# PV summed every three steps, VectorE blocks one by one, FFN values copied out of PSUM early, and fewer steps per run, in a two-layer attention and FFN kernel

## The chip, the cores and the metric

The kernel runs on one core of a Trainium2 chip. A core has a matrix engine (PE, with its weight loads listed apart as PEld), VectorE (DVE), ScalarE (ACT), GpSimd (POOL) and a DMA queue (SP), which run side by side (in the profile of the kernel before PE was busy for 89% of the span, DVE for 65%, ACT for 94% and POOL for 68%) and wait for each other by semaphores. The metric is the device time of one launch in microseconds (us), lower is better. A ratio is the mean time of one kernel's fast runs over the mean time of the other's in the same rounds, so it is not quite the ratio of the medians quoted.

## The reference, cut to what matters

Two layers; each is attention over 2048 tokens with 32 heads of width 16, then an FFN of width 1792, both with a residual and a layernorm in front. The weights are the same in both layers.

```python
x = A_x                                   # 1 x 2048 x 512, bf16
x = x + attention(layernorm(x), wqkv, wo) # 32 heads, Dh = 16, softmax over 2048 keys
x = x + silu(layernorm(x) @ w1) @ w2      # 512 -> 1792 -> 512
x = x + attention(layernorm(x), wqkv, wo)
x = x + silu(layernorm(x) @ w1) @ w2
```

With 32 heads, 2048 queries and 2048 keys, one layer has 134 million exponentials. They are the bulk of the work.

## The kernel before

The kernel is one long software pipeline. Queries go in *chunks* of 512; there are four chunks a layer, so eight in all. A chunk is worked off in eight *runs* of four heads each (four lanes, one per head). In a run each lane has 16 blocks of 128 keys x 512 queries, so a full run has 64 blocks. About three quarters of the blocks get their exponential on ACT, two in each *step*. The others ("VectorE blocks") get an approximation of the exponential: VectorE computes a number whose bits, read as fp16, are a rough exponential (the y tile), and POOL makes two shifted versions of it (the z tiles). PE then sums all three against V and two scaled copies of V. So a run of 24 steps has 48 ACT blocks and 16 VectorE blocks; a run of 23 steps has 46 and 18.

Everything else (layernorm, projections, the output projection, the FFN) is background work: Python generators that yield between pieces. A small model of PE, DVE and ACT decides in which step a piece is put; it is part of the kernel's Python and fixes the instruction order before anything runs. The model knows nothing of POOL.

The parts that the change and the argument touch:

```python
STEPS = {16: (24, 23), 12: (20, 20), 8: (12, 12), 4: (7, 7)}   # keys' blocks: steps
...
t1 = t0 + STEPS[len(kts)][not (0, 1) <= key[0:2] <= (1, 0)]     # key[0:2]: layer, chunk
...
ends = [*range(t0 + 2, t1 - 1, 2), t1]       # PV every two steps
for a, b in zip([t0, *ends], ends):
    pv[b + 1] = list(range(a, b))
```

```python
def emit_d(t, blk):                          # one VectorE block in step t
    s_ps = psum["s"].tile([P, 512], FP32, name="d_ps", tag="sd", bufs=2)
    score(blk, s_ps[:])
    if not pairs or len(pairs[-1]["ds"]) == 2:
        y = dpool.tile([P, 2, 512], U16, name="d_y", tag="y", bufs=Y_BUFS)
        pairs.append(dict(ds=[], y=y))
    ...                                      # nc.vector.tensor_scalar -> one half of y
    if len(pr["ds"]) == 2 or blk == last_d:
        other_terms(t, pr)

def other_terms(t, pr):                      # POOL, once for a pair: 128 x 1024
    for k, (off, _) in enumerate(TERMS):     # two terms
        z = dpool.tile([P, 2, 512], U16, name=f"d_z{k}", tag=f"z{k}")
        nc.gpsimd.tensor_scalar(out=z..., in0=pr["y"]..., scalar1=float(off), scalar2=1.0,
                                op0=ALU.add, op1=ALU.mult)
```

```python
# PV: 'real' groups of four matmuls side by side (starts some 3 ns apart in the trace before);
# 'fill' groups multiply by zeros only to keep PE busy, which is meant to hold its clock (with
# more of them PV by three ran at a clock of 0.991 instead of 0.936, below; FULL_CLOCK = 3
# groups for two steps)
fill = math.ceil(FULL_CLOCK - busy - real) if real > 1 else 0
fill = max(0, min(fill, 2))
...
# FFN: h = w1 part; tanh read from PSUM; multiply reads PSUM and SBUF
h_ps = yield from mm4("h_ps", ..., out=0)
t_sb = tpool.tile([P, 512], FP32, name="t_sb", tag="t")      # one buffer
silu_tanh(h_ps, t_sb[:])                                     # ACT
yield part(0.6, held=True)
silu_mul(ft, h_ps, t_sb[:], hT)                              # VectorE: (t + 1) * h
```

The softmax here doesn't subtract the row's maximum and nothing guards it: scores larger than these inputs give would overflow.

## Time and profile before

| kernel before | |
|---|---|
| median of 4 runs | 1616.74 us (1610.56 to 1624.54) |
| span of the profiled run | 1605.9 us |
| ACT busy | 94% |
| PE busy | 89% |
| POOL busy | 68% |
| DVE busy | 65% |
| mean granted TensorE clock of the profiled run | 0.986 |
| exponentials on ACT, VectorE blocks, POOL z operations | 1552, 992, 992 |

The page's table of busy times, and three of its costliest groups. In a group line the columns are: line of the kernel, engine, operation, output and input tiles, shapes, count, then busy us and mean ns of one, then the idle time of the engine just before them and what ended most of it.

```profile
PE 1436.8 (89%) x12965; PEld 439.9 (27%) x12965; DVE 1036.7 (65%) x1729; ACT 1514.0 (94%) x1671; POOL 1098.4 (68%) x1160
...
L1020 ACT ACTIVATE p_sb<-s_ps 128x1024 bf16<-128x1024 f32 x1552 | 1464.9, 1047 | 47.4 <-PE s_ps L754 26.7
...
L836 PE MATMUL o_ps<-w_qkv,zero 128*32 128x512 bf16 x570 | 113.1, 383 | 0.0
...
L526 ACT ACTIVATE t_sb<-h_ps 128x512 f32<-128x512 f32 x98 | 60.3, 615 | 0.0
```

ACT is the engine that sets the time: 1552 exponentials, 47.4 us of waiting before them in the whole run. The 570 matmuls against a tile named zero are the fillers (some of them only even out a group of four).

The timeline of POOL in the seventh chunk (start us, duration us, engine, line, operation):

```profile
1318.48 1.05 POOL L909 TENSOR_SCALAR d_z_20401<-d_y 128x1024 uint16<-128x1024 uint16 x1
1319.60 1.05 POOL L909 TENSOR_SCALAR d_z_20435<-d_y 128x1024 uint16<-128x1024 uint16 x1
1320.73 1.05 POOL L909 TENSOR_SCALAR d_z_20437<-d_y 128x1024 uint16<-128x1024 uint16 x1
```

One z operation on a pair starts 1.126 us after the one before it (the difference of starts). A 23-step run has nine pairs and two operations for each: 18 x 1.126 = 20.3 us of POOL. ACT needs about 23 x 0.933 = 21.5 us for the run. POOL fits, with little to spare.

The busy time by stretch, for the second and the seventh chunk (columns: stretch, its length, then busy us and count for each engine, then granted clock, DMA share and GB/s):

```profile
core 0: us, PE busy (x) PEld busy (x) DVE busy (x) ACT busy (x) POOL busy (x), PEclk, DMA share, GB/s
222.00:417.00 195.00, 175.02 (x1608) 51.02 (x1606) 126.71 (x214) 186.14 (x207) 138.90 (x145) 0.98 0.09 24
1198.00:1380.00 182.00, 166.07 (x1596) 49.66 (x1592) 129.44 (x211) 178.88 (x199) 152.34 (x149) 0.99 0.09 23
```

In both ACT is nearly full and the clock nearly 1.

### The profile page before, as it was taken

The numbers are of one execution on the slowest core, as the hardware profiler recorded it, in microseconds if no ns is written. First come the engines' busy times: TensorE is split into PE (matmuls) and PEld (weight loads), VectorE is DVE, ScalarE is ACT, GpSimd is POOL, SyncE is SP. The second block draws the span as 40 slices with busy tenths as digits, with TensorE's granted clock in tenths as the row PEclk, the third lists the DMA queues.
The fourth block names the chain that finished last, engine by engine and source line by source line (L and its number), as shares of the span: only waits on it lengthen the run. The fifth ranks groups of instructions, "written<-read, shape, count | busy, mean of one in ns | idle before, by whom it ended". The sixth has DMA issues, their size and how long they took to land.

```text
span 1605.9 us, 33881 instructions
## 1 busy us (share of the span) xinstructions
PE 1436.8 (89%) x12965; PEld 439.9 (27%) x12965; DVE 1036.7 (65%) x1729; ACT 1514.0 (94%) x1671; POOL 1098.4 (68%) x1160
## 2 busy tenths in 40 slices
PE   7889888899988999889998997888988899988988
PEld 3222222222222222222222222322222222222223
DVE  5566657567776668656664453776678667777644
ACT  6999989999999999999999998999999999999982
POOL 3447767677876778668743452788888788888860
PEclk9999999999999999999999998999999999999999
DMA  4000010101100001100011000100011101100011
GB/s 125 14 14 2 8 44 11 28 8 30 28 21 18 11 27 28 28 14 25 11 37 27 11 17 8 30 21 18 12 31 30 28 8 31 31 21 18 11 28 49
DMA packets 83506, 38.62 MB, mean 24 GB/s; under 512 B 63632, under 2 KB 82832, under 8 KB 83344
## 3 DMA queue, kind: packets, MB, share of 16 engines
q1 hardware_dynamic: 83344, 36.46, 8.6%
q8 instruction: 101, 1.65, 0.4%
q14 instruction: 61, 0.50, 0.1%
HBM read 28.57 MB, written 4.19 MB: 20 GB/s over the span
## 4 chain that ended last, share of the span: by engine, by line
ACT 43%; PE 33%; issue 11%; DVE 10%; DMA 1%; SPq 1%; POOL 1%; ACTq 0%; DVEq 0%
ACT p_sb L1020 40%; PE s_ps L754 10%; PE o_ps L836 10%; PE f_ps L586 4%; DVE d_y L889 3%; ACT t_sb L526 2%; PE h_ps L373 2%; DVE hT L529 1%; PE v_ps L373 1%; DVE xn L310 1%; DVE st L301 1%; PE y_ps L373 1%; PE k_ps L373 1%; PE q_ps L373 1%; SPq L414 1%
## 5 line engine op out<-in xcount | busy, mean ns | idle before, releaser
L1020 ACT ACTIVATE p_sb<-s_ps 128x1024 bf16<-128x1024 f32 x1552 | 1464.9, 1047 | 47.4 <-PE s_ps L754 26.7
L889 DVE TENSOR_SCALAR d_y<-d_ps 128x512 uint16<-128x512 f32 x992 | 674.4, 687 | 376.7 <-PE d_ps L754 338.1
L754 PE MATMUL s_ps<-QT,KT 32*128 32x512 bf16 x3104 | 602.8, 387 | 68.8 <-ACT p_sb L1020 62.6
L754 PE MATMUL d_ps<-QT,KT 32*128 32x512 bf16 x992 | 382.6, 386 | 0.5 <-DVE QT L405 0.5
L754 PEld LDWEIGHTS <-KT 32*128 32x128 bf16 x4096 | 160.7, 91 | 653.5 <-issue 640.8
L836 PE MATMUL o_ps<-p_sb,VA 128*32 128x512 bf16 x3104 | 316.0, 395 | 6.9 <-DVE oT L992 2.6
L836 PE MATMUL o_ps<-d_y,VA 128*32 128x512 f16 x992 | 176.0, 382 | 0.0
L836 PEld LDWEIGHTS <-VA 128*32 128x32 bf16 x4096 | 101.1, 94 | 190.5 <-issue 180.8
L586 PE MATMUL f_ps<-w_sb,hT 128*128 128x512 bf16 x392 | 112.8, 383 | 4.8 <-DVE hT L529 4.8
L836 PE MATMUL o_ps<-w_qkv,zero 128*32 128x512 bf16 x570 | 113.1, 383 | 0.0
L529 DVE SCALAR_TENSOR_TENSOR hT<-t_sb,h_ps 128x512 bf16<-128x512 f32 x98 | 67.3, 687 | 37.6 <-ACT t_sb L526 35.4
L836 PEld LDWEIGHTS <-VB 128*32 128x32 f16 x1984 | 75.4, 98 | 29.6 <-issue 6.0
L526 ACT ACTIVATE t_sb<-h_ps 128x512 f32<-128x512 f32 x98 | 60.3, 615 | 0.0
L992 DVE CAST oT<-o_ps 128x512 bf16<-128x512 f32 x63 | 43.1, 684 | 11.8 <-PE o_ps L836 11.7
L301 DVE BATCH_NORM_STATS2 st<-x 128x6 f32<-128x512 bf16 x64 | 43.4, 678 | 1.9 <-DMA x<-in_A_x_dram 1.9
L373 PE MATMUL y_ps<-wo,aT 128*128 128x512 bf16 x128 | 37.4, 394 | 4.3 <-DMA wo<-in_A_wo_dram 3.9
L373 PE MATMUL v_ps<-w_qkv,xnT 128*128 128x512 bf16 x128 | 37.4, 390 | 3.0 <-DVE VA L431 3.0
L373 PE MATMUL q_ps<-xnT,w_qkv 128*128 128x512 bf16 x128 | 38.1, 398 | 1.4 <-DVE KT L389 1.4
L586 PEld LDWEIGHTS <-hT 128*128 128x128 bf16 x392 | 25.6, 97 | 50.0 <-issue 40.2
L373 PE MATMUL k_ps<-xnT,w_qkv 128*128 128x512 bf16 x128 | 36.1, 382 | 2.9 <-DVE xnT L336 0.9
L467 PE MATMUL att<-ident,oT 128*128 128x128 bf16 x256 | 29.8, 223 | 8.6 <-DVE hT L529 8.3
L332 PE MATMUL t_ps<-ident,xn 128*128 128x128 bf16 x256 | 23.4, 226 | 15.3 <-DVE xn L310 14.9
(2269 smaller groups left out, 2149.0 us busy)
## 6 DMA issues: line engine op xcount, KB each, us to landing
wo<-in_A_wo_dram SPq DMA_DIRECT2D x8, 512.0 KB, 3.9
x<-in_A_x_dram SPq DMA_DIRECT2D x7, 512.0 KB, 4.4
QT<-q SPq DMA_DIRECT2D x224, 16.0 KB, 1.8
out_dram<-x SPq DMA_DIRECT2D x16, 128.0 KB, 1.7
w_sb<-in_B_w_dram SPq DMA_DIRECT2D x1, 1792.0 KB, 13.7
w_qkv<-in_A_wqkv_dram SPq DMA_DIRECT2D x3, 512.0 KB, 7.2
x<-in_A_x_dram SPq DMA_DIRECT2D x2, 256.0 KB, 3.1
x_0_113<-x SPq DMA_DIRECT2D x4, 128.0 KB, 1.8
```

Of the source, the lines that this page charges most:

```text
L301: nc.vector.bn_stats(st[:], x_sb[c][:, i, :])
L332: nc.tensor.transpose(t_ps[:, ct, u, :], xns[u][:, ct * P : (ct + 1) * P], ident[:, :])
L373: nc.tensor.matmul(ps, lhsT=lhs(ct), rhs=rhs(ct), start=(ct == 0), stop=(ct == CT - 1))
L467: nc.tensor.matmul(att[:, tq, :, :].rearrange("p j s -> p (j s)"), lhsT=o[:, tq * P : (tq + 1) * P], rhs=ident[:, :], start=(i == 0), stop ...
L526: nc.scalar.activation(t_sb, h_ps, ACT.Tanh, scale=0.5)
L529: nc.vector.scalar_tensor_tensor(out=hT[:, ft, :], in0=t_sb, scalar=1.0, in1=h_ps, op0=ALU.add, op1=ALU.mult)
L586: nc.tensor.matmul(y_ps, lhsT=hT[:, ft, tq * P : (tq + 1) * P], rhs=w2_sb[:, ft, :], start=(ft == 0), stop=(ft == FT - 1),)
L754: nc.tensor.matmul(out, lhsT=KT[L, kt // 4][r, g, (kt % 4) * P : (kt % 4 + 1) * P], rhs=QT[g][r, par, :], start=True, stop=True,)
L836: nc.tensor.matmul(o_tiles[key][32 * j : 32 * j + 32, :], lhsT=lhsT, rhs=rhs, start=(n[j] == 0), stop=stop,)
L889: nc.vector.tensor_scalar(out=pr["y"][:, len(pr["ds"]), :], in0=s_ps[:], scalar1=float(1024 * SCALE * math.log2(math.e)), scalar2=float(10 ...
L992: after.pop()()
L1020: nc.scalar.activation(p_tiles[t][:].rearrange("p a b -> p (a b)"), s_ps[:].rearrange("p a b -> p (a b)"), ACT.Exp, bias=-SHIFT * math.log ...
```

## The change: its intent, and the diff

Four things were changed together. PV is summed every three steps, so that PE switches less often between its tile shapes (in the trace before, at full clock, 512-column matmuls or groups of them start about 0.22 us after one of the same tile shape, and 0.31 to 0.32 us after one of another). VectorE blocks are no longer paired, so that their terms are ready sooner and in smaller pieces. FFN values are copied out of PSUM at once, so that one tanh of 1024 columns can do the work of two of 512. And the runs of the first layer's second and third chunk have 23 steps instead of 24, which takes 16 exponentials from ACT and gives 32 more blocks to VectorE. Here is the core of the diff. Cut are the tighter layout of the scaled V, two xn buffers instead of three, a longer pause before the first output projection, bookkeeping, and the model's changes (it no longer counts the wait of a tanh).

```diff
-    Y_BUFS = 5
-    Z_BUFS = 5
+    D_BUFS = 10
+    D_READY = (1, 3, 4)
+    PV_STEPS = 3
...
-            t1 = t0 + STEPS[len(kts)][not (0, 1) <= key[0:2] <= (1, 0)]
+            t1 = t0 + STEPS[len(kts)][key[0:2] != (0, 3)]
...
-            ends = [*range(t0 + 2, t1 - 1, 2), t1]
+            ends = [*range(t0 + PV_STEPS, t1 - 1, PV_STEPS), t1]
...
-        if not pairs or len(pairs[-1]["ds"]) == 2:
-            y = dpool.tile([P, 2, 512], U16, name="d_y", tag="y", bufs=Y_BUFS)
-            pairs.append(dict(ds=[], y=y))
+        y = dpool.tile([P, 512], U16, name="d_y", tag="y")
...
         for k, (off, _) in enumerate(TERMS):
-            z = dpool.tile([P, 2, 512], U16, name=f"d_z{k}", tag=f"z{k}")
+            z = dpool.tile([P, 512], U16, name=f"d_z{k}", tag=f"z{k}")
             nc.gpsimd.tensor_scalar(
...
-            h_ps = yield from mm4(
-                "h_ps", lambda ct: w[:, ct, :], lambda ct: fT[:, ct, :], out=0
-            )
-            t_sb = tpool.tile([P, 512], FP32, name="t_sb", tag="t")
-            silu_tanh(h_ps, t_sb[:])
-            yield part(0.6, held=True)
-            silu_mul(ft, h_ps, t_sb[:], hT)
+            h_ps = yield from mm4("h_ps", lambda ct: w[:, ct, :], lambda ct: fT[:, ct, :])
+            nc.vector.tensor_copy(out=hT[:, ft, :], in_=h_ps)
+            if ft % 2 == 0 and ft > 0:
+                t_sb = yield from silu_tanhs(hT, ft - 2)
+            elif ft > 1:
+                yield from silu_muls(hT, ft - 3, t_sb)
+        t_sb = yield from silu_tanhs(hT, FT - 2)
+        yield from silu_muls(hT, FT - 2, t_sb)
```

The multiply in `silu_muls` now reads both its inputs, tanh and value, from SBUF; before, the value came from PSUM.

## The prediction

> **What bounds it now.** ACT is busy 94% of the 1605.9 us span (busy table), nearly all of it with 1552 exponentials (costliest groups). In the timeline 14 of them fill 13.06 us: 0.933 us each. A 512-wide FFN tanh (0.60 us busy) adds about 0.5. The wait list gives ACT only some 41 us of waiting for PE's scores. So 1552 x 0.933 = 1448, 98 tanh about 50, waits about 45, 14 us before them and 46 behind. PE is 89% busy, DVE 65%, POOL 68%.

> But POOL is near a limit in the second layer: 151 of 180 us busy between 1020 and 1200 us (busy time by stretch). There a run of 23 exponential steps has 18 VectorE blocks, so 9 pairs, so 18 POOL operations of 128x1024, which the timeline shows 1.126 us apart from start to start when back to back: 20.3 us, against 23 x 0.933 = 21.5.

> **What the change does.**
> - 16 fewer exponentials (23 for 24 steps in two chunks): -15 us of ACT. 32 more VectorE blocks at 0.69 us: +22 us of DVE.
> - 98 tanh of 512 become 49 of 1024 at about 1 us: -5 to -12 us of ACT. 98 copies out of PSUM at 0.69: +67 us of DVE; the multiply now has two SBUF inputs.
> - PV by three steps: 391 fewer matmuls (compiled order), mostly zero fillers, and fewer changes of tile shape on PE; perhaps 10 to 20 us of ACT's waits go.
> - POOL: 992 operations of 128x1024 become 2048 of 128x512.

> About 40 us of gains lie on the critical path, if nothing else binds. The last point does. The 128x136 POOL scalings of V start 0.37 us apart, the 128x1024 ones 1.126: a line through both gives 0.85 ns per element and 0.25 us fixed, so about 0.69 us (estimate) for 512. [...] A 23-step run needs 36: 24.8 us against ACT's 21.5. POOL becomes the bound in five chunks of eight such runs, two of which had 24 steps before. A 24-step run needs 32: 22.1 against 22.4, a tie.

> Sum, in us: start 14; chunk 1: 210; chunks 2 and 3: 288 x 0.69 + 9 of other POOL work = 208 each (before about 190); chunk 4: 189; chunk 5: 210; last three: 203 each (before about 181); tail 46. Total 1694. [...]

> **Prediction: 1700 us, 8 in 10 between 1590 and 1750.** Faster by over 2%: 0.15; within 2%: 0.17; slower: 0.68.

> **What would show it.** POOL operations of 512 starting 0.69 us apart; POOL over 90% busy in chunks 2, 3 and 6 to 8, with steps of about 1.07 us there; PE matmuls on the second and third terms waiting for POOL, ACT waiting for scores behind them. In chunks 1, 4 and 5 steps stay at 0.93 to 0.95 us. Zero fillers fall; tanh pairs take about 1 us.

> **What would make it wrong.** If POOL's fixed cost overlaps between successive operations, so that 512 elements take under 0.60 us, ACT binds again: -15, -10, -15, so about 1575. Between 0.60 and 0.65 the two cancel: within 2%. [...]

The sum is whole: 14 + 210 + 2 x 208 + 189 + 210 + 3 x 203 + 46 = 1694 us, put at 1700 as the forecast. Three passages are cut. The first is a remark on method. The second is an allowance beside the sum, up to 40 us in the POOL-bound chunks for multiplies and POOL delaying each other; the author assumed it, and no trace showed it then. The third is the case over 1750 us that was built on it: a larger delay than that, with DVE falling behind. What the runs measured of this delay stands below (z operations of 0.618 us in the mean, 0.850 us where they overlap a multiply, in the trace after).

## More of the kernel before

The kernel before was run again beside every group of experiments; its median went from 1610 to 1621 us, so the ratios, not the medians, are to be compared between groups.

The profiled run took 1607.7 us and is faster than all four timed ones. In the rounds of the experiments the kernel before had clocks of 0.965 to 0.987, so a clock or a chunk time that is compared with this profile makes a loss look somewhat larger than the ratios do.

## The result, and the profile after

The changed kernel took 1772.13 us in the median of 4 runs (1768.29 to 1778.77), against 1616.74 for the kernel before. The ratio is 1.0963, with a 95% interval of 1.0901 to 1.1025. It is slower, as predicted, but by 9.6% and not 5%, and outside the range of 1590 to 1750.

The lines of the page after that answer to those shown of before:

```profile
PE 1491.9 (84%) x12421; PEld 446.0 (25%) x12574; DVE 1118.4 (63%) x1859; ACT 1513.5 (85%) x1606; POOL 1355.6 (76%) x2216
...
L1019 ACT ACTIVATE p_sb<-s_ps 128x1024 bf16<-128x1024 f32 x1536 | 1457.3, 1034 | 206.9 <-PE d_ps L769 116.0
...
L541 ACT ACTIVATE t_sb<-hT 128x1024 f32<-128x1024 bf16 x49 | 52.4, 1070 | 9.8 <-DVE hT L544 9.8
...
L851 PE MATMUL o_ps<-w_qkv,zero 128*32 128x512 bf16 x115 | 38.7, 438 | 0.0
```

ACT has as much to do as before but waits 206.9 us before its exponentials instead of 47.4. The fillers fell from 570 to 115. A matmul that took 383 ns in the mean takes 438 in that group: the mean clock is lower, 0.901 in this profiled run and 0.986 in that of before.

POOL in the seventh chunk:

```profile
1449.91 0.62 POOL L912 TENSOR_SCALAR d_z_22275<-d_y 128x512 uint16<-128x512 uint16 x1
1450.60 0.62 POOL L912 TENSOR_SCALAR d_z_22277<-d_y 128x512 uint16<-128x512 uint16 x1
1451.30 0.62 POOL L912 TENSOR_SCALAR d_z_22299<-d_y 128x512 uint16<-128x512 uint16 x1
1451.99 0.62 POOL L912 TENSOR_SCALAR d_z_22301<-d_y 128x512 uint16<-128x512 uint16 x1
```

Half the columns take 0.696 us from start to start, not half of 1.126: a line through these two sizes has about 0.27 us for each operation (2 x 0.696 - 1.126) and 0.84 ns for a column, an estimate from these two spacings. It goes on like this, with some 0.08 us between one end and the next start. A 23-step run needs 36 x 0.696 = 25.1 us of POOL; ACT needs 21.5.

The busy time by stretch, for the second, fifth and seventh chunk:

```profile
core 0: us, PE busy (x) PEld busy (x) DVE busy (x) ACT busy (x) POOL busy (x), PEclk, DMA share, GB/s
239.00:450.00 211.00, 176.86 (x1552) 52.62 (x1571) 145.93 (x243) 181.54 (x192) 185.81 (x296) 0.92 0.09 22
865.00:1101.00 236.00, 202.32 (x1523) 57.75 (x1537) 116.88 (x196) 210.49 (x224) 111.08 (x189) 0.86 0.07 18
1315.00:1523.00 208.00, 171.10 (x1513) 49.44 (x1528) 137.61 (x224) 180.69 (x191) 184.75 (x292) 0.92 0.08 20
```

In the seventh chunk POOL shows 184.75 us busy of 208. Its 292 operations also have a gap of about 0.08 us each between end and next start (0.696 less 0.617), 23 us; together that is the whole chunk. PE feels it: summed over the numbered z tiles, PE waited once for POOL's z tiles in the trace of before (0.7 us), and 58 times in the trace after, 61.0 us in all. The fifth chunk is a different matter: POOL is busy for less than half of it, yet it takes 236 us, and its clock is 0.86.

The chunk times below come from counting the starts of the exponentials in the two traces (208, 184 or 192, 184 or 192, 192, 216 and three times 184 steps). "Sum" is the figure that the prediction put in. The times are good to about 1 us, and they set a fast run of before (1607.7 us) against the slowest of the four after (1778.8).

| chunk | before, us | sum predicted | after, us | after less sum |
|---|---|---|---|---|
| 1 | 208.2 | 210 | 225.2 | +15 |
| 2 | 194.9 | 208 | 210.9 | +3 |
| 3 | 191.2 | 208 | 215.4 | +7 |
| 4 | 188.2 | 189 | 198.2 | +9 |
| 5 | 218.9 | 210 | 235.6 | +26 |
| 6 | 181.4 | 203 | 214.5 | +11 |
| 7 | 182.2 | 203 | 208.2 | +5 |
| 8 | 180.3 | 203 | 205.8 | +3 |

The five chunks with 23-step runs (2, 3, 6, 7, 8) were expected to get 95 us longer (1025 less 930) and got 125 longer (1055 less 930). The other three were expected to get 6 shorter (609 less 615) and got 44 longer (659 less 615); against the sum they are 50 over. So most of the loss lies in the chunks where POOL was to bind, though not all of it there need be POOL's, and there is another loss where POOL isn't full.

The clock tells where to look. Cutting both traces into stretches of 3 us, 42 us of the kernel before lie in stretches with a granted clock under 0.7; in the changed kernel it is 321 us. (The expectations below have 39 us for before and 192 us for PV by three alone, from a count that missed a few stretches.) In the fifth chunk one can see how such a stretch begins. These are 2-us stretches of the changed kernel, columns as above:

```profile
1010.00:1012.00 2.00, 1.91 (x21) 0.53 (x20) 0.83 (x2) 1.94 (x3) 0.00 (x0) 1.00 0.00 0
1012.00:1014.00 2.00, 1.31 (x19) 0.33 (x17) 1.13 (x2) 2.00 (x3) 1.23 (x2) 1.00 0.00 0
1014.00:1016.00 2.00, 1.65 (x17) 0.49 (x14) 0.85 (x3) 2.00 (x3) 1.23 (x2) 1.00 0.00 0
1016.00:1018.00 2.00, 1.11 (x11) 0.31 (x12) 0.61 (x1) 2.00 (x3) 1.23 (x2) 1.00 0.00 0
1018.00:1020.00 2.00, 1.36 (x17) 0.30 (x10) 0.85 (x2) 2.00 (x4) 1.13 (x2) 0.93 0.00 0
1020.00:1022.00 2.00, 1.76 (x14) 0.39 (x13) 0.53 (x1) 2.00 (x3) 1.34 (x3) 0.50 0.00 0
1022.00:1024.00 2.00, 1.25 (x12) 0.17 (x8) 0.69 (x1) 1.14 (x3) 0.31 (x1) 0.50 0.03 8
```

The clock record shows more. Cut at those edges into windows of 3.413 us, the window before this loss (1016.32 to 1019.73 us) has PE busy for 2.27 us, 66%. In the traces of before and after, all 54 windows that were followed by a loss of the clock had PE busy for 70% or less; all 770 full-clock windows above that kept it, and so did 46 of those below. The way back was harder: in the trace after, the half clock ended only after windows in which PE was busy for 89% or more (43 times), and it went on after 60 windows with a median of 81%. So a half clock outlasted the light load that came before it.

### The profile page after: what moved, and what is told of

It reads as the page before. It is cut to its first block, busy times and chain, and to the rows that moved or that the text cites. A ratio compares the mean times of both kernels' runs of the same rounds, so it can differ in the third digit from the quotient of the medians.

```text
span 1776.5 us, 33468 instructions
## 1 busy us (share of the span) xinstructions
PE 1491.9 (84%) x12421; PEld 446.0 (25%) x12574; DVE 1118.4 (63%) x1859; ACT 1513.5 (85%) x1606; POOL 1355.6 (76%) x2216
## 4 chain that ended last, share of the span: by engine, by line
PE 34%; ACT 16%; POOL 13%; issue 6%; DVE 5%; DMA 0%; ACTq 0%; DVEq 0%; POOLq 0%
ACT p_sb L1019 15%; PE o_ps L851 12%; PE s_ps L769 12%; PE h_ps L373 3%; PE f_ps L602 3%; DVE d_y L901 2%; DVE hT L544 1%; DVE hT L591 1%; ACT t_sb L541 1%; PE y_ps L373 1%; PE q_ps L373 1%; PE d_ps L769 1%; PE f_ps L655 1%; PE k_ps L373 1%; PE t_ps L332 1%
## 5 line engine op out<-in xcount | busy, mean ns | idle before, releaser
L1019 ACT ACTIVATE p_sb<-s_ps 128x1024 bf16<-128x1024 f32 x1536 | 1457.3, 1034 | 206.9 <-PE d_ps L769 116.0
L769 PE MATMUL s_ps<-QT,KT 32*128 32x512 bf16 x3072 | 620.1, 416 | 166.8 <-ACT p_sb L1019 153.4
L769 PE MATMUL d_ps<-QT,KT 32*128 32x512 bf16 x1024 | 417.7, 416 | 2.0 <-DVE d_y L901 0.8
L851 PE MATMUL o_ps<-p_sb,VA 128*32 128x512 bf16 x3072 | 343.5, 424 | 0.0
L851 PE MATMUL o_ps<-d_y,VA 128*32 128x512 f16 x1024 | 201.2, 413 | 0.2 <-DVE VA L431 0.2
L851 PEld LDWEIGHTS <-VB 128*32 128x32 f16 x2048 | 95.6, 103 | 122.0 <-issue 77.5
L591 DVE CAST hT<-h_ps 128x512 bf16<-128x512 f32 x98 | 67.3, 686 | 50.7 <-PE h_ps L373 47.0
L544 DVE SCALAR_TENSOR_TENSOR hT<-t_sb,hT 128x512 bf16<-128x512 f32 x98 | 75.9, 793 | 7.1 <-ACT t_sb L541 7.1
L541 ACT ACTIVATE t_sb<-hT 128x1024 f32<-128x1024 bf16 x49 | 52.4, 1070 | 9.8 <-DVE hT L544 9.8
L851 PE MATMUL o_ps<-w_qkv,zero 128*32 128x512 bf16 x115 | 38.7, 438 | 0.0
L389 DVE CAST KT<-k_ps 128x512 bf16<-128x512 f32 x32 | 22.0, 688 | 23.1 <-PE k_ps L373 23.0
```

Source lines behind the costliest of these rows:

```text
L389: nc.vector.tensor_copy(out=KT[L, c][:, g, :], in_=k_ps)
L541: nc.scalar.activation(t_sb, h_ps, ACT.Tanh, scale=0.5)
L544: nc.vector.scalar_tensor_tensor(out=hT[:, ft, :], in0=t_sb, scalar=1.0, in1=h_ps, op0=ALU.add, op1=ALU.mult)
L591: nc.vector.tensor_copy(out=hT[:, ft, :], in_=h_ps)
L769: nc.tensor.matmul(out, lhsT=KT[L, kt // 4][r, g, (kt % 4) * P : (kt % 4 + 1) * P], rhs=QT[g][r, par, :], start=True, stop=True,)
L851: nc.tensor.matmul(o_tiles[key][32 * j : 32 * j + 32, :], lhsT=lhsT, rhs=rhs, start=(n[j] == 0), stop=stop,)
```

## The experiments

Every experiment is correct against the reference. From the fifth on, the search that places VectorE blocks keeps its results from one run to the next, because it is slow; with that alone the changed kernel builds to the same program (both were built: 33632 instructions, all equal).

### One part at a time

The first four take the parts apart: the changed kernel with pairs again, and the kernel before with one part of the change each.

**Pairs back, in the changed kernel.** The edit puts the code of before for `emit_d` and `other_terms` back:

```diff
-        y = dpool.tile([P, 512], U16, name="d_y", tag="y")
+        if not pairs or len(pairs[-1]["ds"]) == 2:
+            y = dpool.tile([P, 2, 512], U16, name="d_y", tag="y", bufs=Y_BUFS)
+            pairs.append(dict(ds=[], y=y))
...
+        if len(pr["ds"]) == 2 or blk == last_d:
+            other_terms(t, pr)
```

> The changed kernel with the VectorE blocks in pairs again, so POOL works on 128x1024 as before (1024 blocks, 1024 POOL operations at 1.126 us; 36 blocks' terms of a 23-step run cost POOL 20.3 us, not 25.1). Theory POOL (single blocks make POOL the bound): POOL under 90% everywhere, no matmul waits for POOL for long, 1575 to 1610 us. Theory CLOCK (PV by three and fewer zero fillers let the TensorE clock fall to half, whatever POOL does): clock still 0.90 to 0.93, steps in the first and fifth chunk still 1.08 to 1.09 us, 1640 to 1680 us. Theory DVE (the FFN copies and two-SBUF multiplies): over 1700 us.

Measured: 1710.28 us, ratio to before 1.0571 (1.0527 to 1.0615), clock 0.909. By its time alone this falls in the range of theory DVE, but DVE is 66% busy; by its clock it is theory CLOCK; and no theory covers it whole: it wins back 4 points of the 9.6, and no more. The seventh chunk is still at 201.4 us, without POOL being full (POOL 66% busy in all), and the fifth is unchanged at 235.8. PE's waits for z tiles are gone (under 3 us, from 61.0). So single blocks are one cause, and what is left shows a low clock.

**Single blocks alone, in the kernel before.** The edit is the reverse of the one above.

> The kernel before with single blocks alone (1984 POOL operations of 128x512; PV by two, FFN and steps as before). Theory POOL: the last three chunks, with 23 steps, need 288 x 0.696 = 200 us of POOL each and take 205 to 215 us instead of 181; the 24-step chunks need 178 plus 9 and stay near 190 to 195: 1690 to 1720 us. Theory CLOCK with PV by three as its cause, and theory DVE: 1605 to 1625 us.

Measured: 1694.11 us, ratio 1.0473 (1.0402 to 1.0544), as theory POOL expected. Its last three chunks, the only ones with 23 steps here, took 202.9, 205.4 and 204.4 us. That is the figure of 203 that the prediction had. Chunks with 24 steps stayed between 195 and 198. In the wait list, PE now waits for POOL's z tiles:

```profile
PE o_ps L838 <- POOL d_z L899: 49.0, 64, 1.8
```

(engine and line that waited, what for, us in total, times, longest us). In the trace of before there is one such wait, of 0.7 us.

**PV by three steps alone.**

```diff
-            ends = [*range(t0 + 2, t1 - 1, 2), t1]
+            ends = [*range(t0 + 3, t1 - 1, 3), t1]
```

> The kernel before with PV by three steps alone. Theory POOL: nothing to lose, 1595 to 1620 us. Theory CLOCK: fewer zero fillers and longer gaps, mean clock 0.92 to 0.95 instead of 0.986, the first and fifth chunk 10 to 17 us longer each, 1640 to 1670 us.

Measured: 1660.27 us, ratio 1.0251 (1.0215 to 1.0288), clock 0.936, as theory CLOCK expected. The clock of before in the same rounds was 0.966 to 0.980. 198 us lie in half-clock stretches instead of 42. The first chunk grew by 15 us. The size of the fifth chunk's growth, 5 us, was missed; the last three grew by 6 to 8 each.

**The FFN part alone** (with two xn buffers and the tighter layout of scaled V, to make it fit; the longer pause and the model's changes come with it, and none of these was run apart).

```diff
+            nc.vector.tensor_copy(out=hT[:, ft, :], in_=h_ps)
+            if ft % 2 == 0 and ft > 0:
+                t_sb = yield from silu_tanhs(hT, ft - 2)
+            elif ft > 1:
+                yield from silu_muls(hT, ft - 3, t_sb)
```

> The kernel before with the FFN part alone (values copied out of PSUM, one tanh of 1024 for two of 512, multiplies with two SBUF inputs; xn buffers 2 and the tighter layout of scaled V, to fit). Theory POOL and theory CLOCK: ACT saves up to 10 us, 1600 to 1615 us. Theory DVE: DVE and POOL delay each other, 1640 us or more.

Measured: 1667.98 us, ratio 1.0304 (1.0266 to 1.0343), clock 0.949. Theory DVE was nearest, but not for the reason that it gave: DVE is 67% busy. The timeline at the end of an FFN shows what happens. First VectorE, then POOL, ACT and PE (lines of one window; a time in brackets is idle time before, and what ended it):

```profile
507.14 2.12 DVE L542 SCALAR_TENSOR_TENSOR hT<-t_sb,hT 128x512 bf16<-128x512 f32 x2
510.44 1.29 DVE L542 SCALAR_TENSOR_TENSOR hT<-t_sb,hT 128x512 bf16<-128x512 f32 x2 [1.18 <-ACT t_sb L539]
...
502.84 5.88 POOL L924 TENSOR_SCALAR d_z<-d_y 128x1024 uint16<-128x1024 uint16 x5
513.82 1.04 POOL L924 TENSOR_SCALAR d_z<-d_y 128x1024 uint16<-128x1024 uint16 x1 [5.09 <-DVE d_y L904]
...
506.24 1.06 ACT L1035 ACTIVATE p_sb<-s_ps 128x1024 bf16<-128x1024 f32 x1
509.36 1.06 ACT L539 ACTIVATE t_sb<-hT 128x1024 f32<-128x1024 bf16 x1 [2.06 <-DVE hT L542]
...
511.38 0.39 PE L768 MATMUL s_ps<-QT,KT 32*128 32x512 bf16 x2 [2.54 <-ACT p_sb L1035]
...
512.29 0.61 PE L768 MATMUL s_ps<-QT,KT 32*128 32x512 bf16 x2
```

Two multiplies take 2.12 us while POOL works back to back beside them; the next two, with POOL idle, take 1.29. The next tanh needs the tile that they read, of which there is one. ACT has its instructions in the program's order, and the exponentials behind that tanh wait as well: ACT stands 2.06 us, and the next ones start at 510.32 us, after the tanh at 509.36. PE runs out of score buffers and stands 2.54 us. And then the score matmul takes 0.61 us instead of 0.39: the clock has been halved. It came back some 10 us later. So here a stall of 2 us is followed by some 10 us at half clock; in the trace after, the 43 half-clock stretches that end in it last 8.2 us in the mean.

The traces show that this multiply and POOL delay each other. With the FFN part alone, of 98 multiplies the 63 that overlap a z operation take 994 ns in the mean (longest 1526), the others 684; the z operations that overlap a multiply take 1225 ns, the others 1045. In the trace after, the 88 that overlap take 806 ns (longest 1114), the other 10 take 683. The multiply of before, which reads one input from PSUM, shows no such delay: 687 ns for the 89 that overlap a z operation, 688 for the other 9, and 1047 and 1048 ns for the z operations. How long one waits for the other in a single case isn't shown by these figures.

### Repairs: is it the clock, is it the stall?

**PV by three with more fillers.** The aim of three filler groups was for two steps; the edit aims at 4.5 for three.

```diff
-    FULL_CLOCK = 3
+    FULL_CLOCK = 4.5
...
-        fill = max(0, min(fill, 2))
+        fill = max(0, min(fill, 3))
```

> PV by three alone, as in the run that took 1660 us at a clock of 0.936, but the aim of zero fillers raised from 3 groups in two steps to 4.5 in three (966 zero matmuls instead of 196; before has 570). Theory CLOCK (the half clock is the cost of PV by three): clock 0.97 or more, time in half-clock windows from 192 us to under 60, 1600 to 1630 us. Rival BATCH (larger PV batches hold up the scores whatever the clock): clock recovers, but the time stays at 1650 to 1680 us.

Measured: 1624.23 us, ratio 1.0088 (1.0055 to 1.0121), clock 0.991. Half-clock stretches fell from 198 to 24 us. Matmuls that multiply by zeros, and add work to PE, took the loss from 2.5% to 0.9%. So the clock is most of what PV by three costs. One rival is left: the model counts fillers, so they also shift the background work, and that was not tested apart. Alone PV by three isn't worth anything even then: between exponentials that both start at full clock a step takes 0.998 us, against 0.982 before.

**The FFN part with a pause before its last tanh.** At the end of the loop the last tanh followed at once on the multiplies that free its buffer. The edit lets three steps pass.

```diff
+        yield from pause(3)
         t_sb = yield from silu_tanhs(hT, FT - 2)
```

> The FFN part alone, as in the run that took 1668 us, with a pause of three steps before the last tanh of each FFN, which there follows at once on the multiplies that must first free its only buffer. Theory STALL (ACT stands still for that multiply[...]; PE then idles 2.5 us and loses its clock): ACT's waits of tanh on the multiply fall from 14 us to under 4, 1620 to 1650 us. Rival SPREAD (multiply and POOL delay each other all through the FFN, and PE gets less dense work): still 1655 to 1675 us.

Measured: 1629.66 us, ratio 1.0125 (1.0091 to 1.0158), clock 0.971. The wait of that tanh on the multiply, in the wait list with the FFN part alone and then with the pause:

```profile
ACT t_sb L539 <- DVE hT L542: 14.3, 11, 2.4
```

```profile
ACT t_sb L539 <- DVE hT L542: 1.1, 4, 0.3
```

13 us of waiting removed, about 29 us won (1.79 points of the ratio): the stall counted about double, since the clock went with it (0.949 without the pause, 0.971 with it). This is theory STALL. What remains, 1.2%, isn't explained by a run; 90 us are still in half-clock stretches.

**All three repairs in the changed kernel** (pairs, fillers, pause; PV by three, early copies and 23 steps stay).

> The changed kernel with three repairs: POOL on pairs again, zero fillers for three steps (aim 4.5), a pause of three steps before the last tanh. PV by three, early FFN copies and 23 steps stay. If the three causes are all there is: 1590 to 1620 us, clock 0.97 or more. If something else is left: over 1640 us.

Measured: 1634.74 us, ratio 1.0152 (1.0119 to 1.0185), clock 0.993. The three repairs win back 8.1 of the 9.6 points, but the time is 15 us above the range that was expected. At a clock of 0.993 the last three chunks still take 190 us each, against 181 before. The run with PV by three and fillers had 185 to 188 there, the FFN part with the pause 186 to 189; so each part seems to leave some 5 us per chunk that is hardly the clock (the FFN part with the pause has 0.971). That split was not tested further.

**Fillers and pause, but single blocks.** This leaves POOL alone.

> The changed kernel with zero fillers for three steps and the pause before the last tanh; single blocks stay, so only POOL is left as a cause. Theory POOL as summed in the prediction: chunks 2, 3 and 6 to 8 at 203 to 208 us, the other chunks as before, 1680 to 1710 us in all, clock 0.96 or more. Rival (POOL-bound runs lose the clock by their waits anyway): clock under 0.93 and over 1730 us.

Measured: 1739.49 us, ratio 1.0793 (1.0747 to 1.084), clock 0.965: a miss by 30 us, and a useful one. The time is over the rival's 1730 us, but the clock held, so the rival's cause is wrong. (The profiled run is the slowest of the four, 1751 us.) Chunks 1 and 5, where POOL isn't full, came down to 214.0 and 215.6 us from 225.2 and 235.6, near the sum. Chunks 2, 3, 6, 7 and 8 moved by 6 us at most, most of them upwards: 211.4, 217.6, 208.4, 211.5 and 210.2. They are bound by POOL, with little left for the clock to give. Chunk 4 did not come down either, 200.8 after 198.2; with pairs back as well it took 192.6, so what it lost is mostly POOL's too: the tie that the prediction saw for 24 steps came out as a loss. But they are longer than the 203 to 205 us of the run with single blocks alone. The z operations themselves are longer. These are POOL's z operations of the seventh chunk (stretch, length, busy us and count, clock, DMA), first with single blocks alone, then in the changed kernel:

```profile
1231.00:1436.00 205.00, 178.33 (x290) 0.97 0.08 21
```

```profile
1315.00:1523.00 208.00, 182.90 (x288) 0.92 0.08 20
```

178.33 / 290 = 0.615 us for one, and 182.90 / 288 = 0.635. Over 288 operations that is 5.8 us a chunk, most of what the chunks differ by. The changed kernel has 14 multiplies with two SBUF inputs in such a chunk; the kernel with single blocks alone has none. No run took the multiplies away alone, but the trace after settles it: the 139 z operations that overlap a multiply take 0.850 us in the mean, the other 1909 take 0.618, which is the mean with single blocks alone.

### More work, to take load off POOL

**24 steps in all full runs of the changed kernel.** This gives ACT 40 more exponentials and POOL 160 fewer operations.

```diff
-    STEPS = {16: (24, 23), 12: (20, 20), 8: (12, 12), 4: (7, 7)}
+    STEPS = {16: (24, 24), 12: (20, 20), 8: (12, 12), 4: (7, 7)}
```

> The changed kernel with 24 steps in all full runs: 40 more exponentials (37 us of ACT) and 80 fewer VectorE blocks (160 fewer POOL operations of 0.696 us, 111 us of POOL). Theory POOL: POOL's 22.3 us for a run of 24 ties with ACT's 22.4; the chunks that had 23 steps fall from 206 to 216 us to 192 to 205 each, in all 1700 to 1745 us, faster than the changed kernel in spite of more work. Rival, POOL not the bound: 1800 us or more.

Measured: 1751.11 us in the median of four runs that spread widely (1732.99 to 1752.84), ratio 1.0852 (1.0791 to 1.0913), clock 0.904. 37 us of added exponentials did not make it slower; it looks about 1% faster than the changed kernel (1.0852 against 1.0963, from different rounds, and the intervals just overlap). So the rival is wrong. The gain is smaller than expected (the range was 1700 to 1745 us): 312 us are in half-clock stretches, which points to the clock as the next bound; no run tests that.

### Fewer steps, and a version that beats both

**23 steps in the first layer's second and third chunk alone.**

```diff
-            t1 = t0 + STEPS[len(kts)][not (0, 1) <= key[0:2] <= (1, 0)]
+            t1 = t0 + STEPS[len(kts)][key[0:2] != (0, 3)]
```

> The kernel before with 23 steps in the first layer's chunks 2 and 3 alone: 16 exponentials less. If ACT binds there: 1.0 to 0.99 of before, 8 to 15 us gained. If POOL or PE is too near its limit in these chunks: no gain or a loss.

Measured: 1656.09 us, ratio 1.0264 (1.0227 to 1.03): a clear loss. Yet the two shortened chunks gained just what was hoped: 188.3 and 184.5 us instead of 194.9 and 191.2. Chunk 4 lost 17 and chunk 5 lost 39. The timeline of ACT early in chunk 4 and in chunk 5, and two lines of PE in the last of these gaps:

```profile
640.93 1.02 ACT L1024 ACTIVATE p_sb<-s_ps 128x1024 bf16<-128x1024 f32 x1 [4.05 <-PE s_ps L758]
654.37 1.02 ACT L1024 ACTIVATE p_sb<-s_ps 128x1024 bf16<-128x1024 f32 x1 [12.42 <-PE d_ps L758]
...
804.65 7.48 ACT L1024 ACTIVATE p_sb<-s_ps 128x1024 bf16<-128x1024 f32 x8
839.86 1.02 ACT L1024 ACTIVATE p_sb<-s_ps 128x1024 bf16<-128x1024 f32 x1 [27.73 <-PE s_ps L758]
...
817.25 1.83 PE L373 MATMUL y_ps<-wo,aT 128*128 128x512 bf16 x4 [1.59 <-DVE aT L501]
832.55 1.03 PE L332 MATMUL t_ps<-ident,xn 128*128 128x128 bf16 x8 [2.89 <-DVE xn L310]
```

ACT stands still for 4.05 and 12.42 us in chunk 4, which is what that chunk lost, and for 27.73 us in chunk 5. In that last time the trace has PE on the output projection, query projections, transposes and a key projection, one after another, each waiting for VectorE. It is background work of the first layer that the second layer can't start without, and that had been pushed along by the shorter runs. Read so, the chunk's end is a deadline, for chunk 4 as for the second layer; two runs below test it.

**More fillers in the kernel before,** which its own model doesn't count.

```diff
+        keep = max(fill, min(math.ceil(3.5 - busy - real) if real > 1 else 0, 3))
...
-                for j in range(4 * fill):
+                for j in range(4 * keep):
```

> The kernel before with more zero fillers (aim 3.5 instead of 3, 1124 zero matmuls instead of 570), which the schedule's model doesn't count. Theory CLOCK: the 39 us of half-clock windows, mostly in the fifth chunk, shrink to under 15 and 8 to 18 us are gained. Rival: the fillers delay scores and cost as much.

Measured: 1626.63 us, ratio 1.0079 (1.0046 to 1.0112). A miss: the half-clock stretches didn't shrink (48 us), and the fillers cost 0.8%. In these runs fillers help where much of the clock is being lost (PV by three) and cost where little is.

**Both of the last two together.**

> Both of the last two together, the version that may beat both kernels: 0.98 to 0.99 of before if both gains stand.

Measured: 1664.17 us, ratio 1.0312 (1.0279 to 1.0346). Nearly both losses, added (2.6 and 0.8 points).

**23 steps in the second chunk alone, and PV by three with fillers and 23 steps in both.**

```diff
-            t1 = t0 + STEPS[len(kts)][not (0, 1) <= key[0:2] <= (1, 0)]
+            t1 = t0 + STEPS[len(kts)][not (0, 2) <= key[0:2] <= (1, 0)]
```

> The kernel before with 23 steps in the first layer's chunk 2 alone (8 exponentials less). The run with 23 steps in chunks 2 and 3 gained 13 us in those two and lost 55 in the next two, where ACT once stood still for 27.7 us. Theory DEADLINE (the background work of the shortened chunks is late for the second layer's start): one chunk shortened leaves less work over; if it now fits, 0.993 to 0.997 of before; if it doesn't, a stall of 10 us or more at the start of the fifth chunk and 1.0 to 1.015. Rival (23 steps are too dense for PE by themselves): chunk 2 itself no shorter than before.

> PV by three with more fillers, as in the run at 1.0088, with 23 steps in chunks 2 and 3 as in the change (pairs and the FFN of before). Theory DEADLINE with PV by three making room for the background work: no long stall in the fifth chunk, 13 to 15 us below that run: 0.995 to 1.003 of before. If PV by three doesn't make room: a stall of over 20 us as with 23 steps alone, 1.02 to 1.04.

Measured for 23 steps in one chunk: 1601.74 us, ratio 0.9904 (0.9878 to 0.9931). This is 1% below the kernel before, with an interval below 1, by one changed number. Its second chunk took 187.4 us instead of 194.9, the fifth 221.7 instead of 218.9, and ACT's longest wait for scores in the whole run is 2.0 us. The size is a little better than expected. Eight exponentials less account for some 7.5 us of the 15; its clock was also higher than that of before in the same rounds (0.987 against 0.977 in the mean), and why is open.

Measured for PV by three, fillers and 23 steps in both chunks: 1612.96 us, ratio 0.998 (0.9954 to 1.0006), against 1.0088 without the shorter runs; the fifth chunk took 211.2 us, and ACT's longest wait for scores is 3.7 us. So theory DEADLINE holds in both runs: the stall goes when less is pushed on, or when PV by three makes room for two shortened chunks. What that room consists of was not measured. In the changed kernel these two parts belong together.

## Why the prediction was right or wrong

**POOL would become the bound: right, in mechanism and nearly in size.** What failed is below: the steps on PV by three and on the tanh, and with them the one on chunks 1, 4 and 5. The 0.69 us worked out for 512 columns measured 0.696. The chunk times of 203 us for the last three are what single blocks alone gave (202.9 to 205.4). PE waited for the second and third terms and ACT for scores, as said. The sign to look for, "POOL over 90% busy", was badly chosen: the page showed 87 to 89% in those chunks, since it doesn't count the 0.08 us between operations.

**The multiply with two SBUF inputs: within the size allowed for.** The author had allowed up to 40 us for it outside the central figure, as an assumption that no trace showed then; the size was only shown by the runs. The five POOL-bound chunks came out 30 us above the sum; the longer z operations account for 28 us of it (their time above 0.617 us each, in the trace after). The time did come out over 1750 us, but DVE did not fall behind (63% busy), and the delay stayed inside the 40 us.

**"PV by three steps: ... perhaps 10 to 20 us of ACT's waits go": this step failed, in sign.** Alone it cost 2.5%, about 40 us. The prediction counted the fillers that go away as a saving. They were there to hold the clock, and with the same aim for three steps as for two they no longer did (198 us in half-clock stretches instead of 42); with the aim raised, these fell to 24 us and 1.6 of the 2.5 points came back.

**"98 tanh of 512 become 49 of 1024 at about 1 us: -5 to -12 us of ACT": the tanh was sized right (1.070 us busy), the gain was not there.** Alone the part cost 3.0%. The prediction summed ACT's work and didn't ask what that tanh waits for: its single buffer, held by a multiply that POOL delays (994 ns instead of 684 in the mean with the FFN part alone). A pause of three steps took 1.8 of the 3.0 points away.

**"In chunks 1, 4 and 5 steps stay at 0.93 to 0.95 us": wrong.** They took 1.083, 1.032 and 1.091 us. Even before they had taken 1.001, 0.980 and 1.013; 0.933 is an exponential alone, without tanh and waits. In chunks 1 and 5 the rise is mostly the clock: with fillers and pause they fell to 214.0 and 215.6 us. In chunk 4 it isn't: that stayed at 200.8 and came down to 192.6 only with pairs back.

**16 fewer exponentials, -15 us: the size was right, its condition was missed.** The two chunks gain 13 us, but only if the background work still fits. With PV by three and fillers it does (-1.1 points), without them it costs 2.6%.

Do the parts close the sum? The product of the three costs measured alone and of the gain of fewer steps beside PV by three is 1.0473 x 1.0251 x 1.0304 x (0.998 / 1.0088) = 1.094; measured was 1.0963. That is a check and not a proof: the factors come from different rounds, the last was chosen knowing that PV by three makes room (with the 1.0264 of fewer steps alone the product is 1.135), and the costs don't simply multiply. Fillers and pause won back 1.6 and 1.8 points where each part stood alone, but only 1.7 together in the changed kernel, where five chunks wait for POOL.

Against its own sum of 1694 us the profiled run is 82 us over. About 30 us are in the five POOL-bound chunks, nearly all of it the longer z operations, an effect allowed for outside the sum. About 50 us are in chunks 1, 4 and 5, which it took to be untouched. Of these, fillers and pause give back 31 in chunks 1 and 5: that is the cost of the two terms that it had booked as gains. Chunk 4's 9 are mostly POOL's. The 10 left over in chunks 1 and 5 are a sum set too low; it had 210 for chunk 5, where the kernel before already took 218.9.

## What to carry to other kernels

Before splitting an operation, work out its fixed cost from two sizes in the trace by the distance between starts, multiply by the new count, and compare with the engine's slack in the tightest stretch: here that gave the largest single loss nearly right (203 us a chunk, 202.9 to 205.4 measured). Before removing work from PE, ask whether it held the clock: idling was not free here. All 54 losses of the clock in the traces of before and after followed a window with PE busy for 70% or less, and in the one case measured a short stall upstream was paid about twice (13 us of waiting, 29 us of time). And a software pipeline that is packed by a model has deadlines; a shorter stage gains only if what was hidden behind it still fits.
